# Attention and SwiGLU in one kernel: gate products of twelve chunk pairs as seven block products

## The chip, the cores and the metric

The kernel runs on one core of a Trainium2 chip. A core has a matrix engine (TensorE, PE; its weight loads are listed apart as PEld), three engines for elementwise work (VectorE or DVE, ScalarE or ACT, GpSimd or POOL) and a queue engine for transfers (SyncE or SP). Every engine works through its own instructions in the order in which they were built, and waits on semaphores for the others. The metric is the time of one execution on the device in microseconds (us); lower is better.

## What is computed

Eight batches of eight heads: causal attention over 576 positions of 64 numbers, with a decay from the running sum of log f. The heads of a token, side by side, are the 512 numbers of a row of x; 4608 such rows go through a gated feed-forward block.

```python
def _attn_ref(q, k, v, f):
    scores = scale * np.matmul(q, k.transpose(0, 1, 3, 2))
    cum = np.cumsum(np.log(np.clip(f, 0.0001, 1.0)), axis=-1)
    scores = np.where(causal, -1e9, scores + cum[..., :, None] - cum[..., None, :])
    attn = np.exp(scores - np.max(scores, axis=-1, keepdims=True))
    attn = attn / (np.sum(attn, axis=-1, keepdims=True) + 1e-09)
    return np.matmul(attn, v)

def _moe_ref(x, w_gate, w_val, w_out):          # x: 4608 x 512
    g = x @ w_gate                              # w_gate, w_val: 512 x 1536
    silu = g * (1.0 / (1.0 + np.exp(-g)))
    val = x @ w_val
    return silu * val @ w_out                   # w_out: 1536 x 512
```

Inputs and output are fp32; the kernel multiplies in bf16 and accumulates in fp32.

## The kernel before

**Who decides the order.** The kernel is a list of operations, each with an engine, an estimated duration, the operations it waits for, the buffers it takes and frees, and a key. A planner (`Plan.run`) steps through estimated time; whenever an engine is free it takes the ready operation with the smallest key whose buffers are free, and records its instructions. So each engine's order is fixed when the program is built, from estimates; on the chip an engine that reaches an instruction too early waits there, and everything behind it on that engine waits too. A table `ORDER` overrides the keys of early operations.

**Attention.** Work goes by pairs of heads, 32 in all, four to a batch. Per head: `score` (TensorE, L703), `expo` (ACT, L737), `mask` (POOL, L746), `weigh` (TensorE, L760), `invert` and `scale` (DVE, L767, L772). Then x is written, transposed, into `xT`, a ring that holds six batches: `cross` (an SP transfer that transposes, L790). The head pairs' q and k lie in one of eight slots of `QK`, v in one of three tiles `VB`, loaded through five fp32 tiles `natv`.

**Feed-forward.** The 4608 rows are nine tiles t of 512 tokens (`MT`). For each, twelve chunks fc of 128 hidden columns: `unit` records a gate product (`gate`, L918, four TensorE instructions of 512 columns, one per 128 of the 512 inputs), then on ACT and DVE the SiLU, then a value product (`gate` with `wv`), then on DVE the product of both into `HH` (`times`, L935). Before chunk `ALONE` = (6, 6) the SiLU is tanh on ACT (`tanh`, L922) and a DVE operation (`silu`, L932), since tanh and the softmax's exp share a table of functions on ACT; from there on it is one ACT operation (`whole`, L925), and an operation `turn_table` (L928), recorded in `unit` where (t, fc) equals `ALONE`, switches the table. A tile that crosses the end of the ring of x has its product cut in two: tile 6 in 384 and 128 columns.

**Output products.** From tile 3 on, `finish` computes each half of a tile (128 tokens of each 256) by Strassen's scheme with seven products (`product`, L969) of 256 columns over six pairs of chunks. It needs three sums of `HH` per pair (`sums`, L960, DVE, keys of low priority), and a chain of steps that put the seven products together out of two PSUM banks: `mid_copy` (ACT, L982), `both` (POOL, L989), `more` (DVE, L993), `mid_copy` again, `apart` (POOL, L1014), `close` (DVE, L1017). Then `store` (L1020). The very last half uses four banks and smaller steps (`quarter`, `minus`, `close1`).

**Banks.** PSUM has eight banks: "f" 4 for the feed-forward, "s" 2 for scores, "o" 1, "t" 1. After planned time `WIDE_AT` the feed-forward may take all of them (`F_POOLS`). Attention ends some 90 us before the end of the run; tiles 6, 7 and 8 remain then, TensorE running gates of a tile, its output products, gates of the next.

Of the kernel before, what the change touches and what calls it, by code (L numbers as in the profile page):

```python
# [9 lines left out]
F32 = mybir.dt.float32  # L10
# [6 lines left out]
class Buf:  # L17


    def __init__(self, *pools):  # L20
        self.pools, self.pool, self.i, self.left = pools, None, None, 0


class Op:
# [10 lines left out]
class Plan:  # L35
# [16 lines left out]
    def _takes(self, o, t):  # L52
        got = []
        for b in o.take:
            for n in b.pools:
                name, since, until = (n, 0.0, 1e9) if isinstance(n, str) else n if len(n) == 3 else (n[0], 0.0, n[1])
                if since <= t < until and self.free[name]:
                    got.append((b, name, self.free[name].pop(0)))
                    break
            else:  # L60
                for b2, name, i in reversed(got):
                    self.free[name].insert(0, i)
                return False
        for b, name, i in got:
            b.pool, b.i = name, i
        return True
# [155 lines left out]
def kernel(ctx, tc, q, k, v, f, w_gate, w_val, w_out, out):  # L222
# [42 lines left out]
    natv = [sb(f"natv{i}", [P, H, D], F32) for i in range(NNV)]  # L265
# [15 lines left out]
    def ps(b):  # L281
# [15 lines left out]

    plan = Plan(
        {"f": 4, "s": 2, "o": 1, "t": 1, "qk": NQK, "pt0": NPT0, "pt": NPT, "vb": NVB, "nv": NNV,
         "xn": NXN, "rc": NRC, "th": NTH, "hh": NHH, "su": NSU, "ot": NOT},  # L300
        lambda t: 2.0 if t < TWARM else 1.0,
    )

# [243 lines left out]
    for h, name, i in fixed + [(hqk[FB + p], "qk", 2 + p) for p in range(FB)]:  # L547
        h.pool, h.i = name, i
        plan.free[name].remove(i)
    release = lambda p: 0.0 if p < 2 * FB else PACE0 + min(p - 2 * FB, FB) * PACE_A + max(p - 3 * FB, 0) * PACE  # L550

    def ld_quad(e, b, g, x):
# [322 lines left out]
                    if len(prev) == 2:  # L875
                        x_out(b * FB + r, qb, nq, bx[n, r], prev, kk)

    last_score = []

    def attention(p, key):  # L880
        b = p // FB
        bks, qb, nq = (0, 1, 2, 3), 0, NB
        bx, scaled = Buf("xn"), []
        for j in range(2):
            h = 2 * p + j
            bo, ws, x1 = Buf("o"), [], None
            for m, i in enumerate(bks):
                bs = Buf("s")
                a = op(("PE", mm(*[x[2] for x in BANKS[i]])), score, h, i, bs, after=q_ready[h] + [o_qkz], behind=last_score[-1:], take=[bs], use=[hqk[p]],
                       key=key + 0.5 * j + 0.1 * i, tag=("s", h, i))  # L890
                last_score.append(a)
                x, y = soft(h, i, bs, a, x1, key + 0.5 * j + 0.1 * i)
                if i == 1:
                    x1 = x
                ws.append(weigh_op(h, i, bo, 0, y, ws, m == 0, m == len(bks) - 1, key - 0.3 + 0.5 * j))
            br, a = norm(h, bo, ws, nq, key - 1)
# [122 lines left out]
    def store(e, t0, a, bo, c=slice(0, DM)):  # L1019
        E[e].dma_start(out=out[t0 : t0 + P, c], in_=OT[bo.i][:, a, c])  # L1020

    w_ready = {}
    last_gate = [None]
    tails = []
# [29 lines left out]
        read.append((t0, t0 + n, [g, a]))  # L1054
        return g, m

    read = []
# [28 lines left out]
    def finish(t, t0, key, hs, ms, blended):  # L1086
        G = KF // 2
        us, su = [Buf("su") for _ in range(G)], []
        for g in range(G):
            after = ms[2 * g] + ms[2 * g + 1]  # L1090
            for n in range(3):
                w = (2 if n < 2 else 1) * HALF
                su.append(op({e: f(w) for e, f in SUM_ON[n].items()}, sums, n, hs[g], us[g], after=after + su[-1:] * (n > 0), take=[] if n else [us[g]],
                             use=[hs[g]] + ([us[g]] if n else []), key=SUM_KEY, tag=("sum", t, g, n)))
        for q in range(2):
            bo, bz, bx = Buf("ot"), Buf(*F_POOLS(t)), Buf(*F_POOLS(t))
# [11 lines left out]
                           tag=("fo", t, q, m, n))  # L1108
                return a

            def see(fn, *args, after, n=HALF, psum=True, on=None, take=False):
                return op(on or ("DVE", dve(n, psum)), fn, *args, after=after, take=[bo] if take else [], use=[x for x in args if isinstance(x, Buf) and not (take and x is bo)],
                          key=at, tag=(fn.__name__, t, q))
# [9 lines left out]
            if not last:  # L1123
                a = see(mid_copy, bz, bo, after=[m4] + first, on=("ACT", act(2 * HALF)), take=True)
                m5 = mul(5, bz, [a, m4], 0.4)
                m2 = mul(2, bz, [a, m5], 0.5)
                b = op({e: f(HALF) for e, f in (LAST_ON if end else BOTH_ON).items()}, both, bo, after=[a], use=[bo], key=POOL_KEY, tag=("both", t, q))
                c = see(more, bx, bo, after=[b, m6])
                d = see(mid_copy, bz, bo, after=[b, m2], on=("ACT", act(2 * HALF)))
                m7 = mul(7, bx, [c, m6], 0.6)  # L1130
                b = op({e: f(2 * HALF) for e, f in (LAST_ON if end else APART_ON).items()}, apart, bo, after=[c, d], use=[bo], key=POOL_KEY, tag=("apart", t, q))
                c = see(close, bx, bo, after=[b, m7], n=2 * HALF)
                for a in range(2):
                    send(("SP", 0.7), 1.0, [c], t0 + a * HALF + q * P, a, bo)
                continue
# [4 lines left out]
            m2 = mul(2, bw, [a1, m4], 0.4)  # L1140
# [62 lines left out]


QUICK = 3


def F_POOLS(t):
    return ("f",) + tuple((x, WIDE_AT, 1e9) for x in "sot")


WIDE_AT = 290.0


def fast(n):
# [8 lines left out]
    return 0.15 + n / 460  # L1224


SUM_ON = [{"DVE": fast}, {"DVE": fast}, {"DVE": fast}]
# [133 lines left out]
```

## Time and profile before

| | us |
|---|---|
| median of 3 runs | 379.25 (378.67 to 379.86) |
| the profiled execution | 378.57 |
| its span, first to last instruction | 376.9 |
| granted TensorE clock | 1.000 |

The profile is of one execution. Lines such as L918 are lines of the kernel before. A row of the groups has: line, engine, operation, tiles and shapes, count, then busy us and the mean of one in ns, then the idle time of that engine ahead of it and what ended it. A row of the timeline has start, duration, engine, line, operation. Matmuls overlap in their pipeline, so the duration of one (379 ns) is not its pace. POOL's spans are rough.

### The profile page before, as it was taken

To read this page: it belongs to the slowest core of one execution; us is meant where nothing else is said; L and a number is where in the kernel's file an instruction comes from. 1 tells how busy PE (TensorE), PEld (TensorE's weight loads), DVE (VectorE), ACT (ScalarE), POOL (GpSimd) and SP (SyncE) were. 2 spreads that over 40 slices of the span, in tenths; PEclk is the share of its full clock that TensorE was granted. 3 is DMA by queue.
4 is the path that set the end of the run, shared out by engine and by line. 5 is a ranking of instruction groups with operands and counts; after the bars stand their busy time and mean duration, and the time that the engine had idled before them with its cause. 6 is when DMAs were issued, how large, how long until landed. Compare 5 with 4: busy or idle time off the path is not lost.

```text
span 376.9 us, 9094 instructions
## 1 busy us (share of the span) xinstructions
PE 368.7 (98%) x3427; PEld 233.7 (62%) x3427; DVE 248.9 (66%) x575; ACT 214.3 (57%) x438; POOL 161.4 (43%) x388
## 2 busy tenths in 40 slices
PE   8899999999999999999999999999999999999995
PEld 5667665455565555555685458655887776467464
DVE  7878986177526674499737994598638844753664
ACT  7999952265756754746576467555774433323322
POOL 8897547033633643465376437742462012003000
PEclk9999999999999999999999999999999999999999
DMA  8999998969988998998599999994225003002003
GB/s 147 192 197 195 207 200 151 167 117 176 177 186 169 199 164 151 227 189 183 117 155 206 220 132 165 241 222 95 60 73 93 2 2 111 2 0 89 25 0 114
DMA packets 125178, 52.01 MB, mean 138 GB/s; under 512 B 111838, under 2 KB 119710, under 8 KB 124366
## 3 DMA queue, kind: packets, MB, share of 16 engines
q1 hardware_dynamic: 108638, 36.08, 48.5%
q0 software_dynamic: 16288, 15.14, 27.2%
q8 instruction: 27, 0.44, 0.5%
q10 hardware_dynamic: 208, 0.20, 0.2%
q14 instruction: 17, 0.14, 0.1%
HBM read 38.56 MB, written 17.07 MB: 148 GB/s over the span
## 4 chain that ended last, share of the span: by engine, by line
PE 94%; DVE 2%; ACT 2%; issue 1%; POOL 0%; DVEq 0%
PE ps L918 49%; PE ps L969 14%; PE ps L703 10%; PE ps L976 8%; PE ps L760 8%; PE ps L721 1%; PE ps L777 1%; PE ps L578 1%; PE ps L729 0%; ACT QK L327 0%; ACT PT L737 0%; ACT PTa L737 0%; DVE hh L935 0%; ACT L530 0%; PE ps L1195 0%
## 5 line engine op out<-in xcount | busy, mean ns | idle before, releaser
L918 PE MATMUL ps<-xT,wv 128*128 128x512 bf16 (+2 forms) x496 | 111.8, 352 | 0.0
L918 PE MATMUL ps<-xT,wg 128*128 128x512 bf16 (+2 forms) x496 | 111.6, 352 | 0.0
L737 ACT ACTIVATE PT<-ps 128x384 bf16<-128x384 f32 (+2 forms) x192 | 91.7, 510 | 14.8 <-PE ps L703 9.7
L935 DVE SCALAR_TENSOR_TENSOR hh<-th,ps 128x512 bf16<-128x512 f32 (+1 forms) x112 | 74.5, 667 | 21.1 <-PE ps L918 12.9
L922 ACT ACTIVATE th<-ps 128x512 f32<-128x512 f32 (+1 forms) x82 | 47.2, 577 | 54.2 <-PE ps L918 51.8
L746 POOL TENSOR_SCALAR_AFFINE_SELECT PT<-PT 128x128 bf16<-128x128 bf16 (+1 forms) x192 | 54.1, 288 | 44.1 <-ACT PT L737 38.5
L918 PEld LDWEIGHTS <-wv 128*128 128x128 bf16 x496 | 45.0, 97 | 38.1
L918 PEld LDWEIGHTS <-wg 128*128 128x128 bf16 x496 | 45.1, 97 | 37.9
L932 DVE SCALAR_TENSOR_TENSOR th<-th,ps 128x512 f32<-128x512 f32 (+1 forms) x82 | 53.7, 656 | 19.7 <-ACT th L922 19.5
L703 PE MATMUL ps<-QK 68*128 68x256 bf16 x392 | 64.0, 261 | 0.4 <-ACT PTa L737 0.4
L746 POOL TENSOR_SCALAR_AFFINE_SELECT PTa<-PTa 128x256 bf16<-128x256 bf16 x64 | 26.3, 414 | 81.2 <-ACT PTa L737 80.4
L760 PE MATMUL ps<-VB,PT 128*128 128x65 bf16 x768 | 42.1, 193 | 0.0
L703 PEld LDWEIGHTS <-QK 68*128 68x128 bf16 x392 | 31.5, 97 | 14.0 <-issue 0.6
L760 PEld LDWEIGHTS <-PT 128*128 128x128 bf16 x768 | 34.2, 97 | 9.3 <-POOL PT L746 0.9
L737 ACT ACTIVATE PTa<-ps 128x384 bf16<-128x384 f32 x64 | 30.9, 487 | 15.6 <-PE ps L703 14.8
L767 DVE RECIPROCAL rc<-ps 128x5 f32<-128x5 f32 (+2 forms) x68 | 12.8, 188 | 40.4 <-PE ps L760 40.0
L969 PEld LDWEIGHTS <-su 128*128 128x128 bf16 x360 | 34.8, 97 | 4.6
L960 DVE TENSOR_TENSOR su<-hh 128x512 bf16<-128x512 bf16 (+1 forms) x108 | 36.7, 384 | 0.9
L925 ACT ACTIVATE th<-ps 128x512 f32<-128x512 f32 x30 | 17.9, 596 | 32.1 <-PE ps L918 32.1
L976 PE MATMUL ps<-wo,hh 128*128 128x512 bf16 x144 | 34.8, 379 | 0.0
L772 DVE TENSOR_TENSOR xn<-ps,rc 128x320 bf16<-128x320 f32 (+2 forms) x72 | 32.4, 454 | 2.2
L969 PE MATMUL ps<-wt,su 128*128 128x256 bf16 x216 | 28.8, 272 | 0.0
(97 smaller groups left out, 322.1 us busy)
## 6 DMA issues: line engine op xcount, KB each, us to landing
out_dram<-ot SPq DMA_DIRECT2D x34, 256.0 KB
natv<-in_v_dram SPq DMA_DIRECT2D x25, 256.0 KB
qk_d<-in_q_dram POOLq DMA_DIRECT2D x24, 144.0 KB, 3.6
qk_d<-in_k_dram POOLq DMA_DIRECT2D x24, 144.0 KB, 4.4
wv<-in_moe_w_val_dram POOLq DMA_DIRECT2D x3, 512.0 KB, 10.4
wg<-in_moe_w_gate_dram POOLq DMA_DIRECT2D x3, 512.0 KB, 12.2
wo<-in_moe_w_out_dram POOLq DMA_DIRECT2D x4, 384.0 KB, 13.8
VB<-in_v_dram POOLq DMA_DIRECT2D x7, 128.0 KB, 9.1
```

Source lines behind the costliest of these rows:

```text
L703: nc.tensor.matmul(s[:, c : c + w], QK[:KR, hqk[p].i, 1, j * S + kt * P : j * S + (kt + 1) * P], QK[:KR, hqk[p].i, 0, j * S + q0 : j * S + ...
L737: nc.scalar.activation(place(h, i)[:, OFFS[i] : OFFS[i] + c], ps(bs)[:, :c], AF.Exp, scale=0.125)
L746: nc.gpsimd.affine_select(out=d, in_=d, pattern=pat, compare_op=ALU.is_ge, fill=0.0, base=0, channel_multiplier=-1,)
L760: nc.tensor.matmul(o[:, lo : lo + D + 1], pt[:, c : c + P], VB[hvb[b].i][:, kt, hb, : D + 1], start=first and n == 0, stop=last and n == l ...
L772: nc.vector.tensor_mul(XN[bx.i][:, qb : qb + nq, j], o, r)
L918: nc.tensor.matmul(ps(bf)[:, a:b], w[:, ko, fc * P : (fc + 1) * P], xT[:, ko, at : at + b - a], start=ko == 0 and a == 0, stop=ko == KD - ...
L922: nc.scalar.activation(TH[bt.i][:, :n], ps(bf)[:, :n], AF.Tanh, scale=0.5)
L932: nc.vector.scalar_tensor_tensor(out=t, in0=t, scalar=1.0, in1=ps(bf)[:, :n], op0=ALU.add, op1=ALU.mult)
L935: nc.vector.scalar_tensor_tensor(out=HH[bh.i][:, r, lo : lo + n], in0=TH[bt.i][:, :n], scalar=by, in1=ps(bf)[:, :n], op0=ALU.mult, op1=ALU ...
L960: E[e].tensor_tensor(out=o, in0=x, in1=y, op=f)
L969: nc.tensor.matmul(ps(bf)[:, c * HALF : (c + 1) * HALF], left(g)[:, q * P : (q + 1) * P], right[:, g], start=opens and g == 0, stop=g == K ...
L976: nc.tensor.matmul(ps(bf), HH[hs[g].i][:, r, lo : lo + P], wo[:, 2 * g + r], start=g + r == 0, stop=2 * g + r == KF - 1)
```

## The change

In tiles 6, 7 and 8, four of the six pairs of chunks (pairs 1 to 4 in tile 6, 0 to 3 in 7 and 8; twelve in all) compute their gate by the same seven-product scheme as the output: the two chunks and the two halves of the tokens are the rows and columns of blocks, the two halves of the 512 inputs the inner blocks. Each of the seven products is two TensorE instructions of 256 columns. Their operands are five sums of weight blocks (`wsum`, ten DVE operations of 768 columns, once) and five of x blocks (`xsum`, four DVE steps per tile, more where the ring ends). The value products stay as they were, two chunks of four instructions per pair (`VAL7` is empty).

Per pair the results go, in fp32, through a buffer `CT`: products 3 and 4 into a bank; `c_mid` (ACT); products 1 and 6 into a second bank; `c_both` (POOL); `c_more` (DVE); products 5 and 2 into the first bank; `c_mid` again; product 7; `c_apart` (POOL); `c_close` (DVE). Then two `c_silu` (ACT) and, with the value products, two `h_part` (DVE) in place of two `times`.

The sums lie in memory that attention has done with: `WS` in QK slots 6, 7, 0 and 1, in `natv` and in the third `VB`; `XS` in the other two `VB`; `CT` in QK slots 2 to 5, which are held until the scores of the last four head pairs are done. For this the head pairs are bound to their slots (`Buf.only`).

Also: the third sum of `HH`, 256 wide, of pairs 0 to 4 in tiles 6, 7 and 8 goes from DVE to POOL (`SUM2`); `ALONE` becomes (6, 2); `WIDE_AT` goes from 290 to 283; the first half of the last tile is stored by one transfer in place of two (`store2`); in the very last half product 5 no longer waits for product 2 and `minus` comes earlier on DVE.

```diff
@@ Plan._takes
-                if since <= t < until and self.free[name]:
-                    got.append((b, name, self.free[name].pop(0)))
+                fits = [i for i in self.free[name] if b.only in (None, i)]
+                if since <= t < until and fits:
+                    self.free[name].remove(fits[0])
+                    got.append((b, name, fits[0]))
...
+    held = [Buf("ct") for _ in range(FB)]
+    for p in range(2 * FB, BH // 2):
+        hqk[p].only = (p - 2) % NQK
...
+    CT = [QK[:, 2 + i].rearrange("p w c -> p (w c)")[:, : 4 * MT].bitcast(F32)... for i in range(FB)]
+    XS = [VB[i]... for i in (0, 1)]
+    def wsum(e, v, n, k):
+        (h, x), (i, y), f = (((0, 0), (1, 1), ALU.add), ((0, 1), (1, 1), ALU.add), ((0, 0), (1, 0), ALU.add),
+                             ((0, 1), (0, 0), ALU.subtract), ((1, 0), (1, 1), ALU.subtract))[n]
+        E[e].tensor_tensor(out=WS[v][n][:, k], in0=WQ[v][:, h, x, k], in1=WQ[v][:, i, y, k], op=f)
+    def seven(e, v, t, t0, p, ms, bf):
+        for m in ms:
+            left, right, c, opens = {
+                1: (WS[v][0][:, :, p], 0, 0, True), 2: (WS[v][1][:, :, p], None, 1, False), 3: (w[:, 0, 0, :, p], 1, 0, True),
+                4: (w[:, 1, 1, :, p], 2, 1, False), 5: (WS[v][2][:, :, p], None, 0, False), 6: (WS[v][3][:, :, p], 3, 1, False),
+                7: (WS[v][4][:, :, p], 4, 0, False)}[m]
+            for k in range(2):
+                for a, at, n in [(0, 0, HALF)] if right is not None else raw[m == 5]:
+                    x = XS[t % 2][:, right, k] if right is not None else xT[:, 2 * (m == 5) + k, at : at + n]
+                    nc.tensor.matmul(ps(bf)[:, c * HALF + a : c * HALF + a + n], left[:, k], x, start=opens and k == 0, stop=k == 1, ...)
...
+    def seven_group(v, t, t0, p, kk, after, hb, bc):
+        bz, bx = Buf(*F_POOLS(t)), Buf(*F_POOLS(t))
+        m34 = prod((3, 4), bz, ready, 0, True, hb)
+        a = op(("ACT", act(2 * HALF)), c_mid, bz, bc, after=[m34], ...)
+        m16 = prod((1, 6), bx, ready + [m34], 0.2, True)
+        m52 = prod((5, 2), bz, [a], 0.1)
+        b = op({"POOL": pool2(HALF)}, c_both, bc, after=[a], ...)
+        b = op(("DVE", dve(HALF)), c_more, bx, bc, after=[b, m16], ...)
+        a2 = op(("ACT", act(2 * HALF)), c_mid, bz, bc, after=[m52, b], ...)
+        m7 = prod((7,), bx, [b], 0.3)
+        b = op({"POOL": pool2(2 * HALF)}, c_apart, bc, after=[a2, b], ...)
+        c = op(("DVE", dve(2 * HALF)), c_close, bx, bc, after=[b, m7], ...)
...
+    def pair(t, p, t0, hs, kk, after):
+        g, bz, m52, mid, apart_, done = seven_group(0, t, t0, p, kk, after, [hs[p]], bc)
+        s1 = op(("ACT", act(2 * HALF)), c_silu, bc, True, after=[apart_] + tabled, ...)
+        s2 = op(("ACT", act(2 * HALF)), c_silu, bc, False, after=[done] + tabled, ...)
+            for r in range(2):
+                a = op(("PE", mm(*[MT] * KD)), gate, wv, 2 * p + r, t0, MT, bv, after=[g], take=[bv], ...)
+                m.append(op(("DVE", dve(MT)), h_part, bc, bv, hs[p], r, after=[a, s1, s2] + m, ...))
...
     def ffn(t, t0, n):
         for fc in range(KF):
+            if fc // 2 in GATE7[t]:
+                if not fc % 2:
+                    lg, m = pair(t, fc // 2, t0, hs, key + 100 * fc, [last_gate[0]])
+                    ms += [m, []]
+                continue
...
-                su.append(op({e: f(w) for e, f in SUM_ON[n].items()}, sums, ...
+                su.append(op({e: f(w) for e, f in (SUM_ON[n] if n < 2 or (t, g) not in SUM2 else SUM2_ON).items()}, sums, ...
...
+                if end:
+                    op(("SP", 0.7), store2, t0 + q * P, bo, after=[c], ...)
+                    continue
...
-            m5 = mul(5, bz, [a0, m2], 0.5)
-            m7 = mul(7, bx, [c, m5], 0.6)
+            m5 = mul(5, bz, [a0], 0.5)
+            m7 = mul(7, bx, [c, m5, m2], 0.6)
-            e = see(minus, bz, bo, after=[c, m5])
+            e = see(minus, bz, bo, after=[c, m5], key=-4.5)
...
+SUM2 = [(t, g) for t in (6, 7, 8) for g in range(5)]
+XSUM_KEY = 55000
+GATE7 = [()] * 6 + [(1, 2, 3, 4), (0, 1, 2, 3), (0, 1, 2, 3)]
+VAL7 = [()] * 9
-WIDE_AT = 290.0
+WIDE_AT = 283.0
+WSUM_KEY = (2000, 3000)
+WSUM_AT = (242.0, 283.0)
+SUM2_ON = {"POOL": pool2}
-ALONE = (6, 6)
+ALONE = (6, 2)
```

More of the change, by code (lines that the diff above doesn't have):

```diff
@@ new lines, in mid_of, with ends_of, c_mid, c_both @@
+    def mid_of(bc):
+        return CT[bc.i].rearrange("p a d -> p (a d)")[:, HALF : 3 * HALF]
+    def ends_of(a):
+        return a.rearrange("p a (s d) -> p (a s) d", s=2)[:, 0::3]
+    def c_mid(e, bf, bc):
+        nc.scalar.activation(mid_of(bc), ps(bf), AF.Copy)
+    def c_both(e, bc):
+        c = CT[bc.i]
+        E[e].tensor_tensor(out=c[:, 0, :HALF], in0=c[:, 0, HALF:], in1=c[:, 1, :HALF], op=ALU.add)
+    def c_more(e, bf, bc):
+        c = CT[bc.i]
+        nc.vector.tensor_tensor(out=c[:, 1, HALF:], in0=ps(bf)[:, :HALF], in1=c[:, 0, :HALF], op=ALU.add)
@@ new lines, in c_apart, with c_close, c_silu, h_part @@
+    def c_apart(e, bc):
+        c = CT[bc.i].rearrange("p a (s d) -> p (a s) d", s=2)
+        E[e].tensor_tensor(out=c[:, 0::3], in0=c[:, 0::3], in1=c[:, 1:3], op=ALU.subtract)
+    def c_close(e, bf, bc):
+        c = ends_of(CT[bc.i])
+        nc.vector.tensor_tensor(out=c, in0=ps(bf).rearrange("p (a d) -> p a d", a=2), in1=c, op=ALU.add)
+    def c_silu(e, bc, mid):
+        c = mid_of(bc) if mid else ends_of(CT[bc.i])
+        nc.scalar.activation(c, c, AF.Silu)
+    def h_part(e, bc, bt, bh, r):
+        nc.vector.tensor_tensor(out=HH[bh.i][:, r], in0=CT[bc.i][:, r], in1=ps(bt), op=ALU.mult)
@@ new lines, in seven_group, with prod @@
+    def seven_group(v, t, t0, p, kk, after, hb, bc):
+        bz, bx = Buf(*F_POOLS(t)), Buf(*F_POOLS(t))
+        ready = xsums[t] + wsums[v] + after
+        at, got = -5, sevens[t]
+        def prod(ms, bf, after, k, take=False, hold=[]):
+            o = op(("PE", mm(*[HALF] * 2 * len(ms))), seven, v, t, t0, p, ms, bf, after=after, take=[bf] * take + hold, use=[] if take else [bf],
+                   key=kk + k, tag=("gp" if v == 0 else "vp", t, p, ms))
+            got.append(o)
+            return o
+        m34 = prod((3, 4), bz, ready, 0, True, hb)
+        a = op(("ACT", act(2 * HALF)), c_mid, bz, bc, after=[m34], take=[bc], use=[bz], key=at, tag=("c_mid", t, p))
+        m16 = prod((1, 6), bx, ready + [m34], 0.2, True)
+        m52 = prod((5, 2), bz, [a], 0.1)
+        b = op({"POOL": pool2(HALF)}, c_both, bc, after=[a], use=[bc], key=at, tag=("c_both", t, p))
+        b = op(("DVE", dve(HALF)), c_more, bx, bc, after=[b, m16], use=[bx, bc], key=at, tag=("c_more", t, p))
+        a2 = op(("ACT", act(2 * HALF)), c_mid, bz, bc, after=[m52, b], use=[bz, bc], key=at, tag=("c_mid", t, p))
+        m7 = prod((7,), bx, [b], 0.3)
+        b = op({"POOL": pool2(2 * HALF)}, c_apart, bc, after=[a2, b], use=[bc], key=at, tag=("c_apart", t, p))
+        c = op(("DVE", dve(2 * HALF)), c_close, bx, bc, after=[b, m7], use=[bx, bc], key=at, tag=("c_close", t, p))
+        return m34, bz, m52, a2, b, c
@@ L1092, in finish @@
                 w = (2 if n < 2 else 1) * HALF
-                su.append(op({e: f(w) for e, f in SUM_ON[n].items()}, sums, n, hs[g], us[g], after=after + su[-1:] * (n > 0), take=[] if n else [us[g]],
+                su.append(op({e: f(w) for e, f in (SUM_ON[n] if n < 2 or (t, g) not in SUM2 else SUM2_ON).items()}, sums, n, hs[g], us[g], after=after + su[-1:] * (n > 0), take=[] if n else [us[g]],
                              use=[hs[g]] + ([us[g]] if n else []), key=SUM_KEY, tag=("sum", t, g, n)))
@@ L1224, in pool2 @@
     return 0.15 + n / 460
+WSUM_ON = {"DVE": fast}
+WSUM_KEY = (2000, 3000)
+WSUM_AT = (242.0, 283.0)
+SUM2_ON = {"POOL": pool2}
+ENDS_ON = {"POOL": pool2, "DVE": slow}
 SUM_ON = [{"DVE": fast}, {"DVE": fast}, {"DVE": fast}]
```

88 lines of the change are left out of this document (77 added, 11 removed).

## The prediction

> **What bounds the kernel now.** I read the page's first part, then the chain of waits, then the busy time by stretches, the groups by form and the timeline.
>
> ```profile
> span 376.9 us, 9094 instructions
> PE 368.7 (98%) x3427; PEld 233.7 (62%) x3427; DVE 248.9 (66%) x575; ACT 214.3 (57%) x438; POOL 161.4 (43%) x388
> ```
>
> TensorE is busy for 98% of the span, the next engine for 66%. The chain of waits (start, duration, engine, line) names the same engine from the end of attention onward:
>
> ```profile
> 286.50 19.19 PE ps L918 x168
> 305.70 9.17 PE ps L969 x84
> 314.87 20.72 PE ps L918 x96
> 335.59 9.17 PE ps L969 x84
> 344.76 18.99 PE ps L918 x88
> 363.75 7.87 PE ps L969 x72
> ```
>
> These are the gate and value products (L918) and output products (L969) of token tiles 6, 7 and 8, one behind the other without a hole. So a column taken away there shortens the run, if nothing new makes TensorE wait. Paces: 20.72/96 = 0.2158 us for 512 columns, 9.17/84 = 0.1092 for 256; by that slope 384 cost 0.1625 and 128 cost 0.0559. Tile 6 crosses the end of the ring of x, so its chunk is four times 384 + 128; twelve chunk starts lie between these two rows of the timeline, 10.48/12 = 0.873 us each, which fits:
>
> ```profile
> 288.09 1.04 PE L918 MATMUL ps<-xT,wg 128*128 128x384 bf16 x8
> ...
> 298.57 1.04 PE L918 MATMUL ps<-xT,wg 128*128 128x384 bf16 x8
> ```
>
> The stretches (PE, PEld, DVE, ACT, POOL busy) show what the other engines have left:
>
> ```profile
> 250.00:260.00 10.00, 10.00 (x81) 5.50 (x80) 9.02 (x20) 5.77 (x12) 2.46 (x8) 1.00 0.66 123
> ...
> 290.00:300.00 10.00, 10.00 (x93) 7.05 (x92) 8.93 (x20) 4.71 (x8) 0.00 (x0) 1.00 0.01 2
> ...
> 320.00:330.00 10.00, 10.00 (x48) 4.49 (x46) 7.01 (x15) 3.40 (x6) 0.00 (x0) 1.00 0.01 2
> ```
>
> VectorE is 70 to 90% busy under the gates; GpSimd (POOL) is idle there. The change puts work on both.
>
> **Part 1: the products.** Per pair of chunks the gate loses eight 512-column products: 8 x 0.2158 = 1.727 us (tile 6: 2 x 0.873 = 1.747). It gains fourteen of 256 columns: 14 x 0.1092 = 1.529 us (tile 6, where one of the seven reads x across the ring's end in four pieces of 128: 12 x 0.1092 + 4 x 0.0559 = 1.534). Eight pairs save 0.198 each, four save 0.213: **-2.44 us**. Nothing excludes this part; every stage it touches is on the chain. The 0.873 us above leave 0.056 for a piece of 128. The Trainium skill, TensorE: Matmul & The Clock Gate, section "Back-to-back issue gap", gives about 81 ns for a product of 128 columns in a stream with weight loads, by which (an estimate from that page) the sixteen pieces would take 16 x 0.025 = 0.4 us off the gain; the trace decides against it here.
>
> **Part 2: what follows each product.** Durations from the groups of the last 77 us:
>
> ```profile
> L935 DVE SCALAR_TENSOR_TENSOR hh<-th,ps 128x512 bf16<-128x512 f32 x27 | 18.5, 686 | 12.9 <-PE ps L918 12.4
> L925 ACT ACTIVATE th<-ps 128x512 f32<-128x512 f32 x27 | 16.1, 597 | 30.0 <-PE ps L918 30.0
> L960 DVE TENSOR_TENSOR su<-hh 128x512 bf16<-128x512 bf16 x28 | 10.7, 422 | 0.5
> ...
> L982 ACT ACTIVATE ot<-ps 128x512 f32<-128x512 f32 x10 | 6.0, 597 | 18.6 <-PE ps L969 18.6
> L1014 POOL TENSOR_TENSOR ot<-ot 128x512 f32<-128x512 f32 x4 | 5.1, 1266 | 7.8 <-ACT ot L982 7.8
> L960 DVE TENSOR_TENSOR su<-hh 128x256 bf16<-128x256 bf16 x14 | 4.0, 284 | 0.0
> L1017 DVE TENSOR_TENSOR ot<-ps,ot 128x512 f32<-128x512 f32 x5 | 3.5, 692 | 11.3 <-POOL ot L1014 11.2
> L989 POOL TENSOR_TENSOR ot<-ot 128x256 f32<-128x256 f32 x4 | 2.9, 724 | 45.0 <-ACT ot L982 45.0
> L993 DVE TENSOR_TENSOR ot<-ps,ot 128x256 f32<-128x256 f32 x6 | 2.5, 425 | 5.5 <-POOL ot L989 5.3
> ```
>
> The gate group has the form of the output's seven products, so these rows price it: c_mid as L982, c_both as L989, c_more as L993, c_apart as L1014, c_close as L1017, c_silu as L925, h_part as L935. Per pair, against TensorE's 1.529 + 2 x 0.863 = 3.26 us: ACT 4 x 0.60 = 2.4; DVE 0.43 + 0.69 + 2 x 0.69 + 2 x 0.42 = 3.3, less some overlap of starts; POOL 0.72 + 1.27 and the sum moved to it. That sum (bf16, 256 wide) no row shows on POOL; it lies between DVE's 0.28 and POOL's fp32 0.72, and I take 0.72, the same engine and width. POOL: 2.7. No engine is over 3.26 by much. The handoffs are short:
>
> ```profile
> 310.40 1.27 POOL L1014 TENSOR_TENSOR ot<-ot 128x512 f32<-128x512 f32 x1 [1.95 <-ACT ot L982]
> ...
> 311.70 0.69 DVE L1017 TENSOR_TENSOR ot<-ps,ot 128x512 f32<-128x512 f32 x1 [2.79 <-POOL ot L1014]
> ...
> 363.59 0.60 PE L969 MATMUL ps<-wo,hh 128*128 128x256 bf16 x4
> ...
> 363.86 0.69 DVE L935 SCALAR_TENSOR_TENSOR hh<-th,ps 128x512 bf16<-128x512 f32 x1 [1.04 <-PE ps L918]
> ```
>
> 0.03 from POOL to DVE, 0.27 from TensorE's last column (363.59, where the next product begins) to the reader. In the built order of DVE, c_close of a pair stands just before c_more of the next, so pairs are linked in a loop: c_apart 1.27, c_close 0.69, c_more 0.43, c_mid 0.60, next c_apart: 2.99, with handoffs 3.1. That is under 3.26, so with nothing else the loop costs nothing, covered by the value products of the pair; walking tiles 7 and 8 through the order with these durations leaves 0.1 to 0.8 us between a bank coming free and its next product. This is the cover; anything over 0.2 us in the loop uncovers it.
>
> **Part 3: VectorE and GpSimd together.** On DVE two sums of the pair before stand between c_more and the next c_close, and they come up while c_apart runs on POOL. The trace shows bf16 sums beside POOL only in attention:
>
> ```profile
> 219.51 0.40 POOL L746 TENSOR_SCALAR_AFFINE_SELECT PTa<-PTa 128x256 bf16<-128x256 bf16 x1 [7.21 <-ACT PTa L737]
> ...
> 219.53 0.52 DVE L960 TENSOR_TENSOR su<-hh 128x256 bf16<-128x256 bf16 x1
> ...
> 208.31 1.05 DVE L960 TENSOR_TENSOR su<-hh 128x256 bf16<-128x256 bf16 x3
> ...
> 208.53 0.55 POOL L746 TENSOR_SCALAR_AFFINE_SELECT PT<-PT 128x128 bf16<-128x128 bf16 x1
> ...
> L746 POOL TENSOR_SCALAR_AFFINE_SELECT PT<-PT 128x128 bf16<-128x128 bf16 x128 | 38.6, 303 | 27.0 <-ACT PT L737 22.4
> ```
>
> The 256-wide sum, 0.28 alone, took 0.52 beside a mask of 0.40 that had just begun: it ended 0.14 after the mask did. The mask at 208.53, 0.30 on average, took 0.55 with sums before it. So the two engines wait for each other, one instruction at a time. Whether POOL's two-input fp32 operations do the same no row shows. Bounds for one link: if they don't, 0. If they do and both sums slip in when c_apart ends, c_close starts some 0.5 us late (0.2 for the first, 0.34 for the second), the loop is 3.6, 0.36 over. If POOL's waiting c_both of the next pair gets in between the sums, 0.72 more: 4.3, 1.0 over. There are seven links (three in tile 6, two each in 7 and 8, whose first pair does its c_apart during the output products); the spare bank time takes one in each tile. Four links: 0, **+1.45** or +4.1 us. I take the middle, since the collision is in the rows and its worst order needs c_both to be waiting each time.
>
> **Part 4: the activation table.** Before, the switch to Silu is recorded as an operation of chunk 6 of tile 6 (L928). After, that place is chunk 2, which is computed in a pair that records no switch; so the load stands in ACT's order before the first c_silu, behind three c_mid. It costs
>
> ```profile
> 293.27 1.28 ACT L928 ACT_TABLE_LOAD   x1
> ```
>
> and held nothing up there. After it stands between the first pair's c_apart and its silu, with the second pair's second c_mid behind it, whose bank the third pair needs about 0.7 us after it would come free: bounds 0 and 1.28, I take **+0.5**.
>
> **Part 5: the rest.** The ten 768-wide weight sums are put among the tile-5 chunks, where DVE is 90% busy with low-priority sums; these are pushed behind them and due only at tile 5's output products. DVE also loses the SiLU multiplications of tile 6's chunks 2 to 5. I price both at 0; without the cover the ten cost 10 x 0.55 us by this row, in the upper bound only:
>
> ```profile
> L948 DVE TENSOR_TENSOR wt<-wo 128x768 bf16<-128x768 bf16 x6 | 3.1, 550 | 0.0
> ```
>
> The x sums take two or three 0.42s between pairs and share Part 3's lot. At the end, the joined store leaves SP free a little sooner and the subtraction at L1006 moves ahead of a closing addition; the last store still waits for three DVE operations after the last product:
>
> ```profile
> 372.93 0.42 DVE L1006 SCALAR_TENSOR_TENSOR ot<-ps,ot 128x256 f32<-128x256 f32 x1
> ...
> 373.45 0.43 DVE L1010 TENSOR_TENSOR ot<-ps,ot 128x256 f32<-128x256 f32 x1
> ...
> 373.91 0.38 ACTq L1020 DMA_DIRECT2D out_dram<-ot  x1
> ```
>
> 0, between -0.3 and +0.1.
>
> **Sum**: -2.44 + 1.45 + 0.5 + 0 = -0.5 us. The profiled execution took 378.57 us (span 376.9 and 1.7 around it), so 378.1 for such a one; it was the fastest shown, the median is 379.25, and I forecast 379.25 - 0.5 = **378.7 us**, own range 377.6 to 379.8.
>
> **Rivals.**
> A. The waits of Part 3 fall into spare bank time or don't happen with POOL's fp32 additions; the table load stays: -2.44 + 0.5 = -1.9, **377.3 us** (376.8 if the load hides too). For it: DVE's floating-point instructions with one operand in PSUM (L1017, L935, the c_ steps) keep their 0.69 us throughout, and no row shows a slowed L1014. Against: in the rows above DVE stands idle while L1014 runs (11.2 us of waiting for it), so none of them has a sum beside it.
> B. The other side: the loop of Part 3 in its bad order, in tiles 6 to 8. It decides once a link takes over 3.26 us and the four links together over 1.9; at 4.3 us a link the run is -2.44 + 0.5 + 4.1 = +2.2, **381.4 us**. For it: the mask at 208.53 got in between two sums in just this way. Against: each stall delays the next pair's c_both too, which loosens the order. The Trainium skill says this mechanism outright: SBUF — State Buffer, section "Who interferes with whom", has a VectorE tensor_tensor with both inputs in SBUF contend with GpSimd's reads, the second to come waiting for the whole of the first; by that rule rival B's waits happen at every c_apart. The masks agree with it (0.52 us against 0.28); for POOL's tensor_tensor no run yet shows it.
>
> **Chances.** Forecast 0.40, A 0.33, B 0.27. About 0.3%, 1.14 us, is what a measurement of this kernel can tell from no change. A is faster nearly always (0.31), the forecast a quarter of the time (0.09): faster 0.40. The forecast is within 1.14 otherwise (0.28), with a little of A and B: same 0.33. B gives slower 0.24, the forecast's upper end 0.03: 0.27. The range, into A and B: 376.9 to 381.2.
>
> **What would show it.** In the profile after: the chain's gate stretches of tiles 6, 7, 8 shorter by 0.85, 0.8, 0.8 us where TensorE has no idle time; idle time before the seven products, put down to DVE or ACT, is Part 3 or 4. Sums of over 0.6 us beside c_apart, and c_both over 0.8, show Part 3; constant 0.42 and 0.72 show A. The load should appear before the first c_silu with TensorE idle within 3 us behind it. The prediction is wrong if TensorE idles before tile 6 (weight sums), or if POOL's sums of 256 take over 1 us.

## The result, and the profile after

The changed kernel took 385.32 us (median of 4 runs, 384.61 to 385.60), the kernel before beside it 379.23: ratio 1.0157, interval 1.0136 to 1.0179. So it is 6.1 us slower. The forecast of 378.7 was on the wrong side, and its range ended at 381.2.

The page of the kernel after, first part:

```profile
span 383.8 us, 9272 instructions
PE 368.0 (96%) x3440; PEld 238.4 (62%) x3475; DVE 275.8 (72%) x605; ACT 227.6 (59%) x461; POOL 199.5 (52%) x427
```

TensorE now stands idle. The busy time of TensorE by stretches (length, busy and count, granted clock, DMA) says where; before the change each of these stretches was full:

```profile
240.00:260.00 20.00, 19.89 (x149) 1.00 1.02 197
260.00:280.00 20.00, 18.85 (x231) 1.00 0.44 67
280.00:288.00 8.00, 8.00 (x107) 1.00 0.48 91
288.00:315.00 27.00, 24.47 (x216) 1.00 0.09 26
315.00:345.00 30.00, 29.25 (x204) 1.00 0.10 36
345.00:372.00 27.00, 25.02 (x166) 1.00 0.11 40
```

The idle time is 6.5 us: 1.3 in attention, 2.5 in tile 6 and its output products, 0.75 in tile 7, 2.0 in tile 8. A hole costs 0.16 more than its idle time, because the last product ahead of it counts as busy for 0.38 us where the next would have begun after 0.216. Counted from start to start against the normal pace, nineteen holes of 0.13 to 1.32 us make 9.2: 2.0 in attention, 2.6 among the gates of tile 6, 1.3 in its output products, 0.8 in tile 7, 2.5 in tile 8. With the -2.44 of Part 1 that is +6.8; the span grew by 6.9.

What ended TensorE's waits (waiting operation, releaser, us in total, times, longest), from 240 us on:

```profile
PE ps L926 <- DVE QK L1100: 1.9, 3, 0.9
PE ps L977 <- DVE su L968: 1.5, 2, 1.2
PE ps L1075 <- DVE QK L1092: 1.2, 3, 0.7
PE ps L766 <- POOL PTa L752: 0.5, 1, 0.5
PE ps L766 <- DVE xn L778: 0.4, 1, 0.4
PE ps L1075 <- ACT QK L1084: 0.4, 1, 0.4
```

L926 are the plain gate and value products, L1075 the products of a pair, L977 the output products, L766 the weighting by attention. Nearly all wait for VectorE: for c_close (L1100), c_more (L1092) and the sums over the hidden tile (L968). The timeline of VectorE and GpSimd in tile 8 shows one round of the loop:

```profile
354.68 1.27 POOL L1096 TENSOR_TENSOR QK<-QK 128x512 f32<-128x512 f32 x1 [1.16 <-ACT QK L1084]
355.47 1.63 DVE L968 TENSOR_TENSOR su<-hh 128x512 bf16<-128x512 bf16 x2
356.04 0.78 POOL L1088 TENSOR_TENSOR QK<-QK 128x256 f32<-128x256 f32 x1
356.78 0.85 POOL L968 TENSOR_TENSOR su<-hh 128x256 bf16<-128x256 bf16 x1
357.02 0.68 DVE L1100 TENSOR_TENSOR QK<-ps,QK 128x512 f32<-128x512 f32 x1
357.62 0.41 DVE L1092 TENSOR_TENSOR QK<-ps,QK 128x256 f32<-128x256 f32 x1
358.39 1.29 DVE L1107 TENSOR_TENSOR hh<-QK,ps 128x512 bf16<-128x512 f32 x2 [0.37 <-ACT QK L1104]
358.93 1.27 POOL L1096 TENSOR_TENSOR QK<-QK 128x512 f32<-128x512 f32 x1 [1.30 <-ACT QK L1084]
...
361.27 0.68 DVE L1100 TENSOR_TENSOR QK<-ps,QK 128x512 f32<-128x512 f32 x1
```

Two sums that take 0.75 us with nothing beside them (at 370.5 us of the same trace) take 1.63. They begin beside c_apart (L1096), GpSimd's c_both (L1088) gets in right behind it, and the second sum ends only after that, at 357.10. So c_close starts at 357.02, although c_apart was done at 355.95. From c_close to c_close it is 4.25 us, where TensorE needs 3.26 for a pair.

### The profile page after: what moved, and what is told of

It reads as the page before. It is cut to its first block, busy times and chain, and to the rows that moved or that the text cites. A ratio compares the mean times of both kernels' runs of the same rounds, so it can differ in the third digit from the quotient of the medians.

```text
span 383.8 us, 9272 instructions
## 1 busy us (share of the span) xinstructions
PE 368.0 (96%) x3440; PEld 238.4 (62%) x3475; DVE 275.8 (72%) x605; ACT 227.6 (59%) x461; POOL 199.5 (52%) x427
## 5 line engine op out<-in xcount | busy, mean ns | idle before, releaser
L926 PE MATMUL ps<-xT,wv 128*128 128x512 bf16 (+2 forms) x475 | 109.5, 350 | 2.6 <-DVE QK L1100 1.6
L926 PE MATMUL ps<-xT,wg 128*128 128x512 bf16 (+2 forms) x360 | 85.6, 360 | 0.9 <-DVE QK L1100 0.3
L752 POOL TENSOR_SCALAR_AFFINE_SELECT PT<-PT 128x128 bf16<-128x128 bf16 (+1 forms) x192 | 55.0, 293 | 44.8 <-ACT PT L743 39.6
L930 ACT ACTIVATE th<-ps 128x512 f32<-128x512 f32 (+1 forms) x78 | 44.8, 576 | 50.7 <-PE ps L926 48.3
L926 PEld LDWEIGHTS <-wv 128*128 128x128 bf16 x496 | 45.4, 97 | 36.1 <-issue 2.0
L752 POOL TENSOR_SCALAR_AFFINE_SELECT PTa<-PTa 128x256 bf16<-128x256 bf16 x64 | 26.3, 414 | 79.2 <-ACT PTa L743 78.4
L940 DVE SCALAR_TENSOR_TENSOR th<-th,ps 128x512 f32<-128x512 f32 (+1 forms) x78 | 50.9, 654 | 19.5 <-ACT th L930 19.3
L943 DVE SCALAR_TENSOR_TENSOR hh<-th,ps 128x512 bf16<-128x512 f32 (+1 forms) x88 | 57.9, 660 | 6.9 <-PE ps L926 0.2
L926 PEld LDWEIGHTS <-wg 128*128 128x128 bf16 x368 | 34.0, 97 | 30.1 <-issue 1.5
L968 DVE TENSOR_TENSOR su<-hh 128x512 bf16<-128x512 bf16 (+1 forms) x93 | 46.6, 543 | 0.5
L766 PE MATMUL ps<-VB,PT 128*128 128x65 bf16 x768 | 41.3, 193 | 0.1
L766 PEld LDWEIGHTS <-PT 128*128 128x128 bf16 x768 | 33.5, 97 | 8.7 <-POOL PT L752 1.1
L977 PEld LDWEIGHTS <-su 128*128 128x128 bf16 x360 | 34.6, 97 | 6.7 <-DVE su L968 2.0
L778 DVE TENSOR_TENSOR xn<-ps,rc 128x320 bf16<-128x320 f32 (+2 forms) x72 | 32.4, 454 | 2.2
L984 PE MATMUL ps<-wo,hh 128*128 128x512 bf16 x138 | 33.6, 379 | 0.3
L977 PE MATMUL ps<-wt,su 128*128 128x256 bf16 x216 | 29.0, 272 | 1.5 <-DVE su L968 1.5
L990 ACT ACTIVATE ot<-ps 128x512 f32<-128x512 f32 x22 | 13.1, 597 | 21.7 <-PE ps L977 21.4
```

The lines of the kernel that those rows point to most:

```text
L752: nc.gpsimd.affine_select(out=d, in_=d, pattern=pat, compare_op=ALU.is_ge, fill=0.0, base=0, channel_multiplier=-1,)
L766: nc.tensor.matmul(o[:, lo : lo + D + 1], pt[:, c : c + P], VB[hvb[b].i][:, kt, hb, : D + 1], start=first and n == 0, stop=last and n == l ...
L778: nc.vector.tensor_mul(XN[bx.i][:, qb : qb + nq, j], o, r)
L926: nc.tensor.matmul(ps(bf)[:, a:b], w[:, ko, fc * P : (fc + 1) * P], xT[:, ko, at : at + b - a], start=ko == 0 and a == 0, stop=ko == KD - ...
L930: nc.scalar.activation(TH[bt.i][:, :n], ps(bf)[:, :n], AF.Tanh, scale=0.5)
L940: nc.vector.scalar_tensor_tensor(out=t, in0=t, scalar=1.0, in1=ps(bf)[:, :n], op0=ALU.add, op1=ALU.mult)
```

## Experiments

Times are medians over the kernel before on the same chip, in us; the changed kernel stands at +6.1.

| run | over before | ratio, interval |
|---|---|---|
| no_pairs | +0.1 | 1.0 (0.9984 to 1.0016) |
| weight_sums_only | +1.2 | 1.0033 (1.0022 to 1.0045) |
| late_sums | +6.4 | 1.0159 (1.0126 to 1.0192) |
| late_78 | +6.8 | 1.0182 (1.0162 to 1.0202) |
| no_share | +4.4 | 1.0117 (1.0089 to 1.0146) |
| early_table | +3.3 | 1.0089 (1.0075 to 1.0103) |
| early_table_mult | +5.9 | 1.0153 (1.0137 to 1.0168) |
| no_weight_sums | +4.3 | 1.0121 (1.0099 to 1.0143) |
| two_tiles_late | +2.9 | 1.0077 (1.0054 to 1.0099) |
| two_tiles | +3.2 | 1.0090 (1.0075 to 1.0105) |
| every_other | +0.5 | 1.0010 (0.9995 to 1.0024) |
| spaced_5 | -0.5 | 0.9989 (0.9977 to 1.0000) |
| spaced_5_m7 | -0.45 | 0.9985 (0.9975 to 0.9995) |
| spaced_6_m7 | -0.4 | 0.9985 (0.9974 to 0.9996) |

### What lies outside the pairs, and the weight sums alone

```diff
-GATE7 = [()] * 6 + [(1, 2, 3, 4), (0, 1, 2, 3), (0, 1, 2, 3)]
+GATE7 = [()] * 9
```

> The changed kernel with no pair computed in seven products (so no weight sums and no x sums either); the third sum on GpSimd in tiles 6 to 8, the other banks from 283 us, the joined store and the order of the last block stay. Theory: the loss of 6.1 us sits in the pairs and the weight sums, so this is the time before within 0.4 us, about 379.2. Rival: the edits at the end of the run and the sums on GpSimd cost something of their own: 379.8 or more, with the last product as early as before and a longer stretch behind it.

It came to +0.1. The small edits, the third sum on GpSimd among them, cost nothing as long as no pair uses the engines.

With the same edit, and the weight sums issued all the same:

> The run without pairs, plus the ten weight sums at 242 us, whose result nothing reads. Theory: the four to five holes of TensorE between 262 and 279 us of the changed kernel (2.0 us together) are the weight sums' doing, so this run is 1.5 to 2.5 us slower than the run without pairs, and its holes are the same ones. Rival: the sums only fill VectorE's idle time and the holes come from something that the pairs demand; then it is within 0.5 us of the run without pairs.

+1.2, and four of the changed kernel's five holes there, of the same lengths. Its stretch and its waits (two views):

```profile
260.00:280.00 20.00, 18.92 (x243) 1.00 0.40 67
```

```profile
PE ps L766 <- POOL PTa L752: 0.5, 1, 0.5
PE ps L766 <- DVE xn L778: 0.4, 1, 0.4
```

The theory holds, with a price below the 1.5 to 2.5 expected. In the changed kernel the weight sums run from 247.8 to 261.3 us. The reason shows in VectorE's busy time (third of the engines) in the kernel before and then in the changed one:

```profile
260.00:270.00 10.00, 10.00 (x96) 6.69 (x95) 8.47 (x20) 7.38 (x16) 3.47 (x10) 1.00 0.37 80
```

```profile
260.00:270.00 10.00, 9.30 (x110) 6.34 (x110) 9.58 (x25) 6.64 (x14) 3.14 (x10) 1.00 0.57 69
```

Between 260 and 270 us VectorE goes from 85 to 96%. It was the sums over the hidden tile that were pushed back, as the prediction said; but they then ran between the attention's own steps, and the scaling of a head (L778), which frees a bank that TensorE needs, came late. The wait of 0.5 us that is put down to GpSimd's mask (L752) ends with such a scaling as well: in the changed kernel the mask is done at 263.16 us, the scaling at 263.15.

### The loop of the pairs: work or contention

```diff
-            after = ms[2 * g] + ms[2 * g + 1]
+            after = ms[2 * g] + ms[2 * g + 1] + closes.get(t, [])
```

`closes[t]` is the closing addition of the tile's last pair.

> The changed kernel, with every sum over the hidden tile (tiles 6 to 8) held back until the last pair of its tile has had its closing addition; nothing else moved by hand. Theory (the sums on VectorE and the additions on GpSimd hold each other up inside the loop of the pairs): the closing additions of tile 8 come 3.2 to 3.5 us apart and not 4.25, TensorE's holes among the gates of tiles 6 and 8 shrink from about 4.8 us to under 2, up to 1 us a tile comes back in front of the output products: 382 to 384 us. Rival (the loop's own five steps and their handoffs are too long, contention or not): the closing additions stay 4 us or more apart and the time stays at 385 or more.

The loop did what the theory says. Timeline of VectorE in that run, first the lump of sums behind tile 6, then three closing additions of tile 8:

```profile
308.44 6.39 DVE L968 TENSOR_TENSOR su<-hh 128x512 bf16<-128x512 bf16 x8
...
354.25 0.69 DVE L1100 TENSOR_TENSOR QK<-ps,QK 128x512 f32<-128x512 f32 x1 [0.54 <-POOL QK L1096]
357.47 0.69 DVE L1100 TENSOR_TENSOR QK<-ps,QK 128x512 f32<-128x512 f32 x1 [0.55 <-POOL QK L1096]
360.69 0.69 DVE L1100 TENSOR_TENSOR QK<-ps,QK 128x512 f32<-128x512 f32 x1 [0.55 <-POOL QK L1096]
```

The closing additions are 3.22 us apart, and the holes among tile 8's gates are gone. The time did not follow, since the sums now come in one lump: eight of them took 6.39 us behind tile 6's pairs (0.8 each, with GpSimd's third sums beside them), tile 7's first c_close stood behind them, and TensorE waited 3.13 us. So the time was the rival's, for another reason than the rival gave. To spare tile 6, the same with the sums held back in tiles 7 and 8 alone:

> The changed kernel with the sums over the hidden tile held back behind the pairs in tiles 7 and 8 alone; tile 6 as in the changed kernel. Theory: closing additions of tile 8 3.2 us apart, the 2.4 us of holes among its gates gone, some 0.7 to 1 us given back in front of the output products: 383 to 384 us, and TensorE at full clock throughout since no hole is longer than 1.4 us. Rival (what is taken out of the loop comes back whole in front of the output products, because VectorE has no room behind the pairs): 385 or more.

The rival won on the time. The holes among tile 8's gates went, but the output products of tile 7 waited 2.47 us:

```profile
346.06 0.94 PE L977 MATMUL ps<-wt,su 128*128 128x256 bf16 x7 [2.47 <-DVE su L968]
```

Holding back removes VectorE's work as well as its contention from the loop. The next run tells these two apart: it leaves nearly the same work (0.68 us for 0.75) at the same place, and changes what the work reads.

```diff
+                if t == 8 and (t, g) in again and n < 2:
+                    su.append(op(("DVE", ...), h_part if n == 0 else lambda *a: None, *again[t, g], ...))
+                    continue
```

> The changed kernel with, in tile 8, the two 512-wide sums over the hidden tile of each pair (0.41 us each alone, both inputs in SBUF) replaced at their place in VectorE's order by one repeat of the pair's last multiplication (0.68 us, one input in PSUM); the last output block is not the reference's. The bank of that multiplication is held a little longer. Theory (the loop is long because VectorE and GpSimd lock each other out where both read SBUF): the repeat takes 0.7 us beside GpSimd's work, GpSimd's 256-wide addition stays at 0.73, and closing additions come at most 3.6 us apart. Rival (VectorE's mere work and order make 4.25, whatever its operands): 4 us apart or more.

Timeline of VectorE and GpSimd in tile 8 of that run; L1107 x3 are the two multiplications and the repeat:

```profile
355.64 0.68 DVE L1100 TENSOR_TENSOR QK<-ps,QK 128x512 f32<-128x512 f32 x1
...
357.02 2.01 DVE L1107 TENSOR_TENSOR hh<-QK,ps 128x512 bf16<-128x512 f32 x3 [0.23 <-ACT QK L1104]
357.68 1.27 POOL L1096 TENSOR_TENSOR QK<-QK 128x512 f32<-128x512 f32 x1 [0.71 <-ACT QK L1084]
358.96 0.73 POOL L1088 TENSOR_TENSOR QK<-QK 128x256 f32<-128x256 f32 x1
...
358.98 0.69 DVE L1100 TENSOR_TENSOR QK<-ps,QK 128x512 f32<-128x512 f32 x1
```

Three operations in 2.01 us, c_both at 0.73, closing additions 3.34 apart, and TensorE full from 345 to 372 us. So it is what the sums read, and not their mere work or place, that makes 4.25 us of 3.3 in tile 8. The time gives 1.7 us of the 6.1 for it, from two runs only; in the trace the whole 2.5 us of tile 8's holes are gone. The Trainium skill, SBUF — State Buffer, "Who interferes with whom", has just this rule, for a VectorE instruction with two SBUF inputs against GpSimd's reads; this pair of runs agrees with it (0.75 us became 1.63 with both inputs in SBUF, 0.68 stayed 0.67 with one input in PSUM).

### Tile 6: the table load or VectorE's load

```diff
-ALONE = (6, 2)
+ALONE = (6, 0)
```

> The changed kernel with the table switch recorded at chunk 0 of tile 6 instead of chunk 2, so that the load of 1.28 us runs before the first pair (chunks 0 and 1 then use the Silu table too and lose their two multiplications on VectorE). Theory: the load delays the second pair's second copy, and holes of 0.45 and 0.52 us behind it go: 0.5 to 1.0 us faster than the changed kernel, 384.3 to 384.8. Rival (the loop at 4.25 us sets those holes, the load falls into it): within 0.3 us of 385.3.

It gained 2.8 us, far more than either theory said. The edit also takes two multiplications of 0.68 from VectorE, so they were put back:

> The run with the early table, with the two multiplications of chunks 0 and 1 of tile 6 put back on VectorE (they multiply a value that is already a SiLU, so the hidden values of these two chunks are not the reference's). It tells the load's share from theirs. Theory (the load on the path costs most of the 3.1 us): within 0.5 us of the run with the early table, 382.2 to 382.8. Rival (1.4 us of VectorE work less ahead of the first pair brought the gain): 384 or more.

The rival won: with the load out of the way and the multiplications back, the time is +5.9. TensorE's busy time from 288 to 315 us, early_table and then early_table_mult:

```profile
288.00:315.00 27.00, 26.27 (x238) 1.00 0.07 21
```

```profile
288.00:315.00 27.00, 23.86 (x214) 1.00 0.09 26
```

Moving the load alone gained 0.2 us, which is within the noise (1.0153 against 1.0157). The 1.4 us of VectorE work at the start of tile 6 go with 2.6 us of time. But the planner also orders VectorE anew between these two: in early_table one pair's two sums happen to miss GpSimd's additions (0.79 us), while in early_table_mult an x sum (L1062) of 0.41 us takes 1.48 right ahead of a closing addition, for which TensorE waits 1.24 us. How much of the 2.6 is order and how much work stays open. The last run of this group leaves out the weight sums:

```diff
+                    continue
                     wsums[v] += [op(...
-                1: (WS[v][0][:, :, p], 0, 0, True), ...
+                1: (w[:, 0, 0, :, p], 0, 0, True), ...
```

> The changed kernel without the ten weight sums: the products that should read them read the unsummed weights, so the gates of the pairs are not the reference's. Everything else stays. Theory (VectorE's backlog from the weight sums, on top of its 95% around 250 to 270 us, reaches into tile 6 and makes holes there as well as in attention): the 2.0 us of holes in attention go, and of tile 6's 3.9 us at least 2 as well: 381 to 382.5 us. Rival (tile 6 has its holes from the loop of its own pairs and the table load): 383.5 to 384.3, tile 6's holes 3.5 us or more.

+4.3, between the two. Its stretches:

```profile
260.00:280.00 20.00, 20.00 (x221) 1.00 0.35 84
...
288.00:315.00 27.00, 25.34 (x227) 1.00 0.04 7
315.00:345.00 30.00, 28.95 (x203) 1.00 0.10 36
345.00:372.00 27.00, 25.11 (x169) 1.00 0.11 41
```

Attention is full again, tile 6 loses 1.7 of idle time in place of 2.5, tile 7 a little more than before. So the weight sums' backlog makes about a third of tile 6's idle time. The rest belongs to its pairs: with none in tile 6 (two_tiles, below) 0.5 us is left in this stretch, though the weight sums run there. How it divides between the pairs' loop, the x sums and the table load no run shows.

### Fewer pairs, and pairs set apart

With pairs 0 to 3 of tiles 7 and 8 alone, and the weight sums in tile 6 (`WSUM_AT` 284):

> Pairs 0 to 3 of tiles 7 and 8 in a row, weight sums in tile 6, the sums not held back. Theory: eight pairs save 1.6 us; the loop at 4.25 us costs some 2.5 us in tile 8 and 0.2 to 0.5 in tile 7, as in the changed kernel, and the output products wait less than with the sums held back (2.9 us there): 379.5 to 380.5. Rival (contention in the loop is not what costs): the time of the run with the sums held back, 381.8, or more.

> As the run with late sums, but no pairs in tile 6, and the weight sums in tile 6 (from 284 us on) in place of tile 5: eight pairs. Theory: the attention stage is as before the change, tile 6 hides 5.5 us of weight sums since VectorE has 30% free and GpSimd is idle there, and eight pairs save 8 x 0.198 = 1.58 us: 377.7 to 378.7. Rival: the weight sums stall tile 6 as they stalled tile 5, or the loop of the pairs is over its period without the sums too: 379.5 or more.

+3.2 and +2.9: both missed what the theory gave, and in both the rival's number came. The attention stage is whole again. In two_tiles tile 8 loses as much as in the changed kernel; with the sums held back it loses nothing among its gates, and the output products of tile 7 wait 2.1 us for the sums instead. So contention is only a part of it: with four pairs in a row there is no place left for the sums. So a plain pair was put behind each pair:

```diff
-GATE7 = [()] * 6 + [(1, 2, 3, 4), (0, 1, 2, 3), (0, 1, 2, 3)]
+GATE7 = [()] * 6 + [(), (0, 2, 4), (0, 2, 4)]
```

> Pairs in seven products only in tiles 7 and 8, and there every other one (0, 2, 4), each followed by a plain pair; weight sums in tile 6 from 284 us on; the sums over the hidden tile as in the changed kernel. Theory (what costs is that consecutive pairs are linked in a loop that sums and additions stretch to 4.25 us, against 3.26 of TensorE): with a plain pair between, the loop has 6.7 us, its stretching falls into spare bank time, and six pairs save 6 x 0.2 = 1.2 us: 377.4 to 378.2, with no hole of TensorE among the gates. Rival (each pair costs more elsewhere than it saves, wherever it stands): 379 or more.

+0.5: the time is the rival's, 1.2 us above the range expected, but 2.8 us faster than two_tiles with two pairs less. One of the two waits left among its gates, in the timelines of VectorE and of TensorE:

```profile
351.21 2.09 DVE L968 TENSOR_TENSOR su<-hh 128x512 bf16<-128x512 bf16 x3
353.23 0.41 DVE L1092 TENSOR_TENSOR QK<-ps,QK 128x256 f32<-128x256 f32 x1
```

```profile
353.69 0.38 PE L1075 MATMUL ps<-VB,VB 128*128 128x256 bf16 x2 [0.36 <-DVE QK L1092]
```

Product 7 waits for c_more, which stands behind three slowed sums. Three more runs put the weight sums behind the sums over the hidden tile, and all three sums of a pair on VectorE; the second and third also put product 7 behind the next gate chunk:

```diff
-WSUM_KEY = (2000, 3000)
+WSUM_KEY = (52000, 53000)
-SUM2 = [(t, g) for t in (6, 7, 8) for g in range(5)]
+SUM2 = []
...
-        m7 = prod((7,), bx, [b], 0.3)
+        m7 = prod((7,), bx, [b], 200.5)
```

> Pairs 2, 4 of tile 7 and 0, 2, 4 of tile 8, each followed by a plain pair; weight sums from 284 us on but behind the sums over the hidden tile in VectorE's choice; all three sums over the hidden tile on VectorE. Theory: the 0.64 us hole in front of tile 6's output products goes (the weight sums no longer stand ahead of the sums that they need), the sums wait less for GpSimd, and five pairs save 1.0 us: 377.9 to 378.5 where before is 379.0. Rival (VectorE is full under the gates, so that what is pushed back there comes up in front of a product elsewhere): 379 or more.

> As spaced_5, and the seventh product of each pair is put behind the first gate chunk of the next pair, since the trace of every_other showed TensorE waiting for VectorE's addition in front of it (0.36 and 0.52 us). Theory: the holes in front of it go and nothing waits for its later closing: 377.7 to 378.2. Rival (the pair's banks and its silu come free later and the holes move to the value products): no faster than spaced_5.

> As spaced_5_m7 with pair 0 of tile 7 too: six pairs. Theory: another 0.2 us, 377.5 to 378.0. Rival: the weight sums are not ready for tile 7's first pair, whose products then wait: slower than spaced_5_m7 by 0.3 us or more.

The three can't be told from one another: 0.4 to 0.5 us faster than before, with intervals that just leave out 1 or touch it. spaced_5 came to the upper end of what was expected; the last two missed it by 0.3 and 0.6 us, and spaced_5_m7 is no faster than spaced_5, as its rival had it. The runs from spaced_5 on change several things at once against every_other, so what each of these brought is not shown. In the trace of spaced_6_m7 the saving is whole. First and last group of products of the stretch in question, in the kernel before and in spaced_6_m7:

```profile
240.50 0.71 PE L969 MATMUL ps<-wt,su 128*128 128x256 bf16 x5
...
372.10 0.82 PE L969 MATMUL ps<-wt,su 128*128 128x256 bf16 x6
```

```profile
240.55 0.71 PE L977 MATMUL ps<-wt,su 128*128 128x256 bf16 x5
...
371.32 0.82 PE L977 MATMUL ps<-wt,su 128*128 128x256 bf16 x6
```

131.60 against 130.77 us. In between, the stretch from 288 to 315 us is all that has idle time left, 0.11 us; counted from start to start, spaced_6_m7 has 0.36 us of holes more than before. 0.83 + 0.36 = 1.19 = 6 x 0.198. The medians show only half of the 0.83; the ratio's interval, 0.15 to 1.0 us faster, holds it.

## Why the prediction was wrong

**Part 1, the products: right.** The last fences show the 0.198 us a pair.

**Part 2, the loop without waits: right.** 3.1 us was forecast, under TensorE's 3.26; it ran at 3.22 with the sums away and 3.34 with other work in their place, and TensorE had no hole among tile 8's gates in either. The sentence "No engine is over 3.26 by much" hid the trouble, though: VectorE's 3.3 us, from durations without contention, already filled a pair, and the sums were counted in. Four pairs in a row leave no time in which a delay could be made up (late_78, two_tiles_late).

**Part 3, VectorE and GpSimd: the mechanism right, the size wrong.** The step that failed is "I take the middle, since the collision is in the rows and its worst order needs c_both to be waiting each time". In two of tile 8's three rounds c_both was waiting: GpSimd takes it up 0.1 us after c_apart, between the two sums. In the third, GpSimd's own sum (L968), which the change had moved there, took that place. The bound of 4.3 us a round was the value (4.26, 4.25 and 4.18). "the spare bank time takes one in each tile" failed too: it left one link to pay for in tile 8, but three lost 2.4 us, and the spare bank time took only some 0.5. In tile 7 rounds of 4.24 and 3.98 us left holes of 0.4 us among the gates; why tile 7 had more time to spare no run shows. Rival B's mechanism was the one that ran, at the price that it gave for a round, but it held only the pairs' own loop. The signs named beforehand came: two sums at 1.63 us, c_both at 0.78 to 0.92.

**Part 4, the table load: the wait right, its worth open.** +0.5 was taken. TensorE's wait within 3 us of the load came: it is the one for L1084 above, 0.4 us, at 296.5 us with the load at 293.6. With the load moved it is gone, but VectorE's other order brought other waits, and the time fell by 0.2 us only (early_table_mult), which is within the noise.

**Part 5: wrong.** The step that failed is "these are pushed behind them and due only at tile 5's output products", from which the 0 follows ("I price both at 0"). The weight sums cost 1.2 us alone and 1.75 within the change. The sign named for it, TensorE idle before tile 6, came, with 1.3 us. The cover named, low-priority sums that can wait, was there; but what waits is not gone. It came up between attention's scalings, in a stage where VectorE had 1.0 to 1.5 us free in ten and was given 5.5 more, and it went on into tile 6, whose idle time is 2.5 us with the weight sums and 1.7 without. Each stage was priced by the loop of a pair; none was priced by the sum of what VectorE had to do in it. The late sums in front of tile 6's output products (1.3 us) were in no term either. The end of the run was right: no_pairs shows no loss.

**The sum.** -2.44, then 2.0 in attention, 3.9 in tile 6, 0.8 in tile 7, 2.5 in tile 8. The forecast had +1.95 for all of that.

## What to carry to other kernels

Add up, stage by stage, everything that an engine must do there before and after the change. Here, where VectorE was 85 to 96% busy, low-priority work was only postponed, and it came back in front of something that was due. Where VectorE has instructions with two SBUF inputs beside GpSimd's, cost them as one engine, in the order in which they come up: here 0.75 us became 1.63. A cheaper form with a long chain behind it did far better where plain work stood between two uses of it (+0.5 us, and -0.4 with the sums moved) than back to back (+3.2).

## What the hardware showed besides

The 3.13 us wait in late_sums cost more than itself. Stretches of TensorE there (granted clock is the column behind the count):

```profile
312.00:314.00 2.00, 0.36 (x4) 1.00 0.00 0
314.00:316.00 2.00, 0.51 (x3) 0.83 0.00 0
316.00:318.00 2.00, 2.00 (x7) 0.50 0.00 0
318.00:320.00 2.00, 2.00 (x16) 0.82 0.00 0
```

When TensorE went on at 315.5 us it ran at half clock for some 3 us, about 1.5 us lost on top. The wait of 2.47 us in late_78 left the clock at 1.00. The Trainium skill, TensorE: Matmul & The Clock Gate, "What's actually happening", says that the clock halves after an idle window of about 3.4 us and comes back after as long of work. The trace agrees in the rate and the return; here 3.13 us of idle time, 3.29 if counted from the pace of the last product, were enough. No run was made for this alone, so where the limit lies stays open.
